# Seven products of quarters for the second matrix product of seven blocks, and a new order of steps

## The chip, the cores and the metric

The kernel runs on one core of a Trainium2 chip. The metric is the device time of one execution in microseconds (us), taken as the median of several runs. The core has a TensorE (PE; its weight loads are shown apart, as PEld), a VectorE (DVE), a ScalarE (ACT), a GpSimd (POOL) and a SyncE (SP), which here only issues transfers. Each engine works through its own queue of instructions in order, and waits on semaphores for the others. Memory on the chip is SBUF (128 partitions) and PSUM (eight banks of 512 float32 per partition), into which TensorE writes.

## The reference

```python
batch, n_heads, seq, head_dim = (8, 8, 576, 64)
scores = scale * np.matmul(q, k.transpose(0, 1, 3, 2))
gamma = 1.0 - 2.0 ** (-5.0 - np.arange(H, dtype=np.float32))
Dmat = np.where(rel >= 0, gamma[:, None, None] ** rel[None, :, :], 0.0)
attn = np.matmul(scores * Dmat[None, :, :, :], v)
x = attn.transpose(0, 2, 1, 3).reshape(B * S, H * D)      # 4608 x 512
h = x @ w_in                                              # 512 x 2048
s = np.sin(alpha * h)
g = h + s * s / (alpha + 1e-09)
out = g @ w_out                                           # 2048 x 512
```

A decaying attention without softmax over 8 batches of 576 positions feeds a two-layer network with a sine between its layers. Inputs and output are float32; the kernel multiplies in float16 with float32 sums.

## The kernel before

The 4608 rows of x are cut into nine blocks of 512. Block n below 8 holds the first 512 positions of batch n; block 8 holds the last 64 positions of all batches. (The title's and the text's blocks go from 0 to 8.)

For each batch the attention goes in chunks of 128 positions. `load` brings tiles of 256 positions, 512 KB each, to SBUF (for k and v of batches from `HALVED` = 5 on as four transfers), `cast` scales them by powers of gamma and rounds to float16, `turn` with `take` (batches 0 and 1, on TensorE and through PSUM) or `crossed` (a transposing DMA, batches 2 to 7) puts the head dimension on the partitions. `outer` makes the sums of k times v of the chunks, `evict`, `evict_bank` or `take_sum` bring them to SBUF, `more` and `to_state` carry the decayed state from chunk to chunk. `scores`, `masked` and `values` do the part inside a chunk, `add_states` adds what earlier chunks bring, and `keep` writes the result as float16, turned, into the block's x. `values` is made in two parts for two row halves of the array, and between them stands a wait: a drain of TensorE in batches 0 to 3, and a relay from there on (`told`: an empty instruction on POOL that waits for the first part, and for which the second waits). Class `Ends` does the same for the last 64 positions.

The network goes over 16 units of 128 hidden columns for each block. `project` (four matmuls of 512 columns) makes h of one unit in a PSUM bank, `sine` (ACT) makes the sine of it, `square` (DVE, ACT or POOL) squares it, and `product` (DVE) makes g = h + square times inverse of alpha as float16 in `gT`. `gemm2(n, u)` is a quarter of the sum for 128 rows of the output: four matmuls with a [128, 128] piece of g as weights and 512 columns of w_out moving, so 16 calls and 64 matmuls for a block. After four of them `finish` copies the bank to SBUF and stores it in two transfers of 64 rows each, because the rows of x stand in another order than the output's (even positions first, then odd).

The order of all steps is written out by hand up to block 3 and then made by loops over the units, with the second product of block n - 1 between the projections of block n, and the attention of block n + 1 at fixed units. PSUM is shared under fixed tags ("h0" to "h2", "op", and pairs "m0", "m1"), SBUF under tags with a few buffers each (six for `raw`): a load waits until a buffer is free. Dummy matmuls (`keep_busy`) stand at the start.

```python
for fk in range(4 * part, 4 * part + 4):
    matmul(
        ops[n, c, cols.start][:, cols], gT[n][:, fk, c * P : (c + 1) * P], w_out16[:, fk, cols],
        start=(fk == 0), stop=(fk == FC - 1), skip_group_check=True,
    )
```

Of the kernel before, what the change touches and what calls it, by code (L numbers as in the profile page):

```python
# [10 lines left out]
F32 = mybir.dt.float32  # L11
F16 = mybir.dt.float16
ADD = mybir.AluOpType.add
MULT = mybir.AluOpType.mult


@with_exitstack
def kernel(
# [10 lines left out]

# [9 lines left out]
    NBLK = NT // 512  # L44
    HALVED = 5
# [19 lines left out]
    work = ctx.enter_context(tc.tile_pool(name="w", bufs=1))  # L65
    psum = ctx.enter_context(tc.tile_pool(name="p", bufs=1, space=bass.MemoryType.PSUM))

    ident = const.tile([P, P], F16, tag="ident", bufs=1)
    mask = const.tile([P, 8 * 64], F16, tag="mask", bufs=1)
    cn = const.tile([P, 68], F32, tag="cn", bufs=1)  # L70
# [3 lines left out]
    eye = const.tile([16, 16], F32, tag="eye", bufs=1)  # L74
    alpha_r = const.tile([FC, P], F32, tag="alpha_r", bufs=1)
    alpha_t = const.tile([P, FC], F32, tag="alpha", bufs=1)
    inva = const.tile([P, FC], F32, tag="inva", bufs=1)
    w_in16 = const.tile([P, KT, FF], F16, tag="w_in16", bufs=1)
    w_out16 = const.tile([P, FC, 512], F16, tag="w_out16", bufs=1)
    sS = const.tile([P, B, 4, D], F16, tag="sS", bufs=1)  # L80
    xS = const.tile([P, KT, 512], F16, tag="xS", bufs=1)
# [4 lines left out]

    V, A_, G_ = nc.vector, nc.scalar, nc.gpsimd

    def load_w_in(g):
        cols = slice(g * 512, (g + 1) * 512)  # L90
        nc.gpsimd.dma_start(w_in16[:, :, cols], w_in_r[:, :, cols])

    def load_w_out(g):
        nc.gpsimd.dma_start(w_out16[:, 4 * g : 4 * g + 4, :], w_out_r[:, 4 * g : 4 * g + 4, :])
# [4 lines left out]
    def copy(eng, d_, s_):  # L99
        if eng is nc.scalar:  # L100
            eng.copy(d_, s_)  # L101
        else:
            eng.tensor_copy(d_, s_)  # L103

    raw = {}
    half = {}
    T = {}

    def load(b, nm, p):
        if p < 2 and b >= HALVED and nm != "q":  # L110
            t_ = work.tile([P, H, 2 * D], F32, tag="raw", bufs=6, name=nm + "32")
            for g in range(2):
                for r in range(2):
                    s0 = 256 * p + 128 * g + 64 * r
                    nc.sync.dma_start(  # L115
                        t_[halves(g), :, r * D : r * D + D], src[nm][b, :, s0 : s0 + 64, :].rearrange("h i d -> i h d")
                    )
        elif p < 2:
            t_ = work.tile([P, H, 2 * D], F32, tag="raw", bufs=6, name=nm + "32")
            nc.sync.dma_start(  # L120
                t_, src[nm][b, :, 256 * p : 256 * p + 256, :].rearrange("h (i r) d -> i h (r d)", r=2)
            )
        else:
            if b % 2 == 0:
                raw[b, nm, 2] = work.tile([P, H, D], F32, tag="raws", bufs=3, name=nm + "s32")
            t_ = raw[b - b % 2, nm, 2]
            nc.sync.dma_start(t_[halves(b % 2)], src[nm][b, :, 512:576, :].rearrange("h i d -> i h d"))
        raw[b, nm, p] = t_

    nbuf = {"k": 4, "q": 3, "v": 4}  # L130

    def cast(b, nm, p, eng, ys=(0, 1)):
        t_ = raw[b, nm, p]
        if (b, nm, p) not in half:
            if p < 2:
                d_ = work.tile([P, 16 * D], F16, tag=nm + "16", bufs=nbuf[nm], name=nm + "16")
                d_ = (
                    d_.rearrange("p (h r d) -> p h r d", r=2, d=D)
                    if nm == "v"
                    else d_.rearrange("p (a r t d) -> p a r t d", a=4, r=2, t=2)  # L140
                )
            elif nm == "v":
                d_ = work.tile([P, H, D], F16, tag="vs16", bufs=B // 2, name="vs16")
            else:
                d_ = work.tile([P, 4, 2, D], F16, tag="qks16", bufs=2, name=nm + "s16")
            half[b, nm, p] = d_
        dst = half[b, nm, p]
        if p == 2:
            if nm == "v":
                copy(eng, dst.rearrange("p h d -> p (h d)"), t_.rearrange("p h d -> p (h d)"))  # L150
            else:
                eng.tensor_tensor(  # L152
                    dst.rearrange("p a t d -> p t a d"),
                    t_.rearrange("p (t a) d -> p t a d", t=2),
                    fac_s[nm].rearrange("p (t a) -> p t a", t=2).unsqueeze(3).to_broadcast([P, 2, 4, D]),
                    MULT,
                )
        elif nm == "v":
            h0, h1 = 4 * ys[0], 4 * ys[-1] + 4
            copy(  # L160
                eng,
                dst[:, h0:h1].rearrange("p h r d -> p (h r d)"),
                t_[:, h0:h1].rearrange("p h x -> p (h x)"),
            )
        else:
            a0, a1 = 2 * ys[0], 2 * ys[-1] + 2
            n = 2 * (a1 - a0)
            eng.tensor_tensor(  # L168
                dst[:, a0:a1].rearrange("p a r t d -> p t (a r) d"),
                t_.rearrange("p (t a) x -> p t a x", t=2)[:, :, a0:a1].rearrange("p t a (r d) -> p t (a r) d", r=2),  # L170
                fac["halved k" if nm == "k" and b >= HALVED else nm]
                .rearrange("p (t x) -> p t x", t=2)[:, :, 2 * a0 : 2 * a1]
                .unsqueeze(3)
                .to_broadcast([P, 2, n, D]),
                MULT,
            )

    def new_T(b, nm, p):
        if (b, nm, p) not in T:
            T[b, nm, p] = (  # L180
                work.tile([P, 8, P], F16, tag=nm + "T", bufs=4, name=nm + "T")
                if p < 2
                else work.tile([P, 4, P], F16, tag=nm + "Ts", bufs=B // 2, name=nm + "Ts")
            )
        return T[b, nm, p]

    def crossed(b, p, nms="kq"):
        for nm in nms:
            x = half[b, nm, p]
            x = x.rearrange("p a r t d -> p (a r t d)") if p < 2 else x.rearrange("p a t d -> p (a t d)")  # L190
            nc.sync.dma_start_transpose(new_T(b, nm, p), x)

    trs = {}

    def turn(b, nm, p, tag, ys=(0, 1)):
        if (b, nm, p) not in trs:
            trs[b, nm, p] = psum.tile([P, 1024], F16, tag=tag, bufs=1, name="tr")
        tr, x = trs[b, nm, p], half[b, nm, p]
        for a in range(2 * ys[0], 2 * ys[-1] + 2):
            for r in range(2):  # L200
                matmul(  # L201
                    tr[:, 256 * a + 128 * r : 256 * a + 128 * r + 128],
                    x[:, a, r].rearrange("p t d -> p (t d)"),
                    ident,
                    start=(a == 0 and r == 0), stop=True, is_transpose=True, skip_group_check=True,
                )

    def take(b, nm, p, eng, ys=(0, 1)):
        d_ = new_T(b, nm, p).rearrange("p x n -> p (x n)")
        cols = slice(512 * ys[0], 512 * ys[-1] + 512)  # L210
        copy(eng, d_[:, cols], trs[b, nm, p][:, cols])

    def quads(firsts, seconds):
        return [(f, s) for s in seconds for f in firsts]

    matmul = nc.tensor.matmul

    open_turns = []

    def change_rows(key):  # L220

        if key in open_turns:
            nc.tensor.drain()
            open_turns.clear()
# [9 lines left out]
    def told(last, eng):  # L234

        mark = eng.nop()
        order(mark, last)
        return mark

    class Attention:  # L240
        def __init__(self, b):
            self.b = b
            self.halved = b >= HALVED
            self.both = {}
            self.o = {}
            self.ret = {}
            self.sc = {}
            self.kv = {}
            self.tiles = {}
            self.mark = {}  # L250

        def tile(self, name, shape, dtype, bufs):
            if name not in self.tiles:
                self.tiles[name] = work.tile(shape, dtype, tag=name, bufs=bufs, name=name)
            return self.tiles[name]

        @property
        def x(self):
            xs[self.b] = self.tile("xT", [P, KT, 512], F16, 3)
            return xs[self.b]  # L260

        @property
        def kvs(self):
            return self.tile("kvs", [P, 4, 4, D], F32, 1)

        def state_of(self, c):
            return self.tile("s16", [P, 3, 4, D], F16, 2)[:, c] if c < 3 else sS[:, self.b]

# [957 lines left out]
```

## Time and profile before

| what | us |
|---|---|
| median of 3 runs (308.53 to 311.25) | 309.3 |
| the profiled execution, its span | 309.4 |
| first projection begins | 25.4 |
| TensorE's last matmul ends | 305.9 |
| ScalarE busy in 144 sines | 97.1 |
| VectorE busy in 144 products (g) | 106.2 |
| TensorE busy in `gemm2`, 592 matmuls | 142.4 |

In a profile a line such as "L562 PE MATMUL ops<-w_out,gT 128*128 128x512 f16 x592 | 142.4, 374" names the line of the kernel, the engine, the operation, what is written from what, the shape, how many there were, and then the busy time in us and the mean of one in ns. After a second bar stands the time that the engine sat idle just before these instructions, and for what. Matmuls are pipelined, so the mean of one is longer than the time from one to the next; the latter is read from the starts. In a timeline a line begins with start and length in us. In a table of windows a line has the stretch, its length, the busy time and number of instructions of PE, PEld, DVE, ACT and POOL, the granted clock of TensorE, the share of time that the DMA engines were busy (over 1 where transfers overlap), and GB/s.

### The profile page before, as it was taken

The numbers are of one execution on the slowest core, as the hardware profiler recorded it, in microseconds if no ns is written. First come the engines' busy times: TensorE is split into PE (matmuls) and PEld (weight loads), VectorE is DVE, ScalarE is ACT, GpSimd is POOL, SyncE is SP. The second block draws the span as 40 slices with busy tenths as digits, with TensorE's granted clock in tenths as the row PEclk, the third lists the DMA queues.
The fourth block names the chain that finished last, engine by engine and source line by source line (L and its number), as shares of the span: only waits on it lengthen the run. The fifth ranks groups of instructions, "written<-read, shape, count | busy, mean of one in ns | idle before, by whom it ended". The sixth has DMA issues, their size and how long they took to land.

```text
span 309.4 us, 7922 instructions
## 1 busy us (share of the span) xinstructions
PE 296.4 (96%) x3257; PEld 150.9 (49%) x3257; DVE 207.4 (67%) x298; ACT 180.7 (58%) x286; POOL 138.4 (45%) x154
## 2 busy tenths in 40 slices
PE   6669999999999999999999999999999999999995
PEld 4546555554544544454445444544454454444443
DVE  1596799989859888666866586576656746655600
ACT  1434983766544766675677567756774456555411
POOL 5690774589449587759149722990030000000000
PEclk9776999999999999999999999999999999999999
DMA  7999999699497788987788788885431111111132
GB/s 227 335 215 217 278 260 247 160 247 303 90 289 213 88 190 183 272 140 171 161 226 209 179 163 192 230 199 132 101 72 39 34 36 36 35 34 37 42 89 73
DMA packets 115540, 49.84 MB, mean 161 GB/s; under 512 B 69792, under 2 KB 111024, under 8 KB 115504
## 3 DMA queue, kind: packets, MB, share of 16 engines
q1 hardware_dynamic: 110912, 44.97, 60.0%
q0 software_dynamic: 4224, 4.19, 8.1%
q8 instruction: 25, 0.41, 0.6%
q10 hardware_dynamic: 368, 0.18, 0.3%
q14 instruction: 11, 0.09, 0.1%
HBM read 36.74 MB, written 9.44 MB: 149 GB/s over the span
## 4 chain that ended last, share of the span: by engine, by line
PE 84%; DMA 3%; POOL 3%; SPq 3%; DVE 2%; ACT 1%; issue 1%; DVEq 0%; ACTq 0%; POOLq 0%
PE ops L562 39%; PE hps L519 37%; DMA q<-in_q_dram 3%; PE o L384 3%; PE sc L342 2%; SPq L115 2%; POOL q L168 1%; PE kv L282 1%; DVE s L316 1%; DVE ret L354 1%; PE o L406 1%; SPq L120 1%; ACT s_t L527 1%; POOL k L168 1%; PE tr L201 0%
## 5 line engine op out<-in xcount | busy, mean ns | idle before, releaser
L562 PE MATMUL ops<-w_out,gT 128*128 128x512 f16 (+2 forms) x592 | 142.4, 374 | 0.3 <-ACT kvs L101 0.2
L543 DVE SCALAR_TENSOR_TENSOR gT<-ss_t,inva,hps 128x512 f16<-128x512 f16 x144 | 106.2, 745 | 53.1 <-ACT ss_t L536 46.1
L527 ACT ACTIVATE s_t<-hps,alpha_t 128x512 f16<-128x512 f32 x144 | 97.1, 686 | 71.3 <-PE hps L519 68.8
L519 PE MATMUL hps<-xT,w_in 128*128 128x512 f16 (+1 forms) x544 | 127.7, 370 | 0.0
L519 PEld LDWEIGHTS <-w_in 128*128 128x128 f16 x608 | 59.1, 99 | 64.5 <-issue 0.9
L562 PEld LDWEIGHTS <-gT 128*128 128x128 f16 x592 | 56.2, 98 | 64.3 <-issue 0.7
L538 DVE TENSOR_TENSOR ss_t<-s_t 128x512 f16<-128x512 f16 x72 | 42.2, 587 | 19.5 <-ACT s_t L527 18.8
L536 ACT ACTIVATE ss_t<-s_t 128x512 f16<-128x512 f16 x62 | 38.8, 631 | 0.9
L354 DVE TENSOR_TENSOR ret<-sc,mask 128x1024 f16<-128x1024 f32 (+1 forms) x32 | 35.1, 1118 | 1.9 <-PE sc L342 1.8
L168 POOL TENSOR_TENSOR k<-k,cn 128x1024 f16<-128x1024 f32 (+1 forms) x13 | 22.1, 1699 | 25.0 <-DMA k<-in_k_dram 20.7
L101 ACT COPY osb<-ops 128x512 f32<-128x512 f32 (+1 forms) x34 | 19.7, 582 | 22.0 <-PE ops L562 20.6
L168 POOL TENSOR_TENSOR q<-q,cn 128x1024 f16<-128x1024 f32 (+1 forms) x16 | 27.2, 1708 | 10.1 <-DMA q<-in_q_dram 10.0
L538 POOL TENSOR_TENSOR ss_t<-s_t 128x512 f16<-128x512 f16 x10 | 10.8, 1083 | 19.5 <-ACT s_t L527 10.7
L101 ACT CAST xT<-o 128x1024 f16<-128x1024 f32 (+1 forms) x14 | 13.2, 958 | 7.9 <-PE o L406 7.8
L324 POOL TENSOR_TENSOR kvs<-s,kvs 128x256 f32<-128x256 f32 x22 | 16.1, 730 | 3.1 <-ACT kvs L101 1.4
L103 POOL CAST v<-v 128x1024 f16<-128x1024 f32 (+1 forms) x10 | 12.2, 1234 | 9.5 <-DMA v<-in_v_dram 8.4
L519 PE MATMUL hps<-xS,w_in 128*128 128x512 f16 x64 | 16.4, 379 | 0.0
L323 POOL TENSOR_TENSOR s<-kvs,cn 128x256 f32<-128x256 f32 x22 | 14.3, 651 | 0.3
L152 POOL TENSOR_TENSOR ks<-ks,cn 128x512 f16<-128x512 f32 x4 | 4.2, 1041 | 22.0 <-PE o L384 22.0
L384 PE MATMUL o<-ret,v 64*64 64x128 f16 (+1 forms) x512 | 11.9, 226 | 1.3 <-DVE ret L354 0.7
L342 PE MATMUL sc<-qT,kT 64*64 64x128 f16 (+1 forms) x512 | 10.9, 221 | 1.9 <-DVE ret L354 1.9
L316 POOL TENSOR_TENSOR s<-kvs,cn 128x256 f16<-128x256 f32 x19 | 12.2, 646 | 1.1 <-ACT kvs L101 0.5
(59 smaller groups left out, 142.3 us busy)
## 6 DMA issues: line engine op xcount, KB each, us to landing
out_dram<-osb SPq DMA_DIRECT2D x70, 128.0 KB, 2.4
q<-in_q_dram SPq DMA_DIRECT2D x16, 512.0 KB, 6.2
k<-in_k_dram SPq DMA_DIRECT2D x10, 512.0 KB, 8.2
v<-in_v_dram SPq DMA_DIRECT2D x10, 512.0 KB, 6.2
k<-in_k_dram SPq DMA_DIRECT2D x24, 128.0 KB, 3.1
v<-in_v_dram SPq DMA_DIRECT2D x24, 128.0 KB, 3.2
w_in<-in_moe_w_in_dram POOLq DMA_DIRECT2D x4, 512.0 KB, 11.3
w_out<-in_moe_w_out_dram POOLq DMA_DIRECT2D x4, 512.0 KB, 9.8
```

The source lines that it names most:

```text
L101: eng.copy(d_, s_)
L168: eng.tensor_tensor(dst[:, a0:a1].rearrange("p a r t d -> p t (a r) d"), t_.rearrange("p (t a) x -> p t a x", t=2)[:, :, a0:a1].rearrange( ...
L324: nc.gpsimd.tensor_tensor(self.kvs[:, c], s32, self.kvs[:, c], ADD)
L342: matmul(sc[halves(g), t, c : c + n], kT[halves(t), 2 * a + r, halves(g)], qT[halves(t), 2 * a : 2 * a + 2, 64 * g + i0 : 64 * g + 64], st ...
L354: nc.vector.tensor_tensor(ret.rearrange("p t (z x) -> p (t z) x", z=2)[:, :, 0:n], sc.rearrange("p t (z x) -> p (t z) x", z=2)[:, :, 0:n], ...
L384: made.append(matmul(o[t][halves(e), c : c + 128].rearrange("p (r i) -> p r i", r=2)[:, :, i0:64], v16[halves(g), 4 * t + 2 * x + e, r, :] ...
L519: matmul(hps_of[n, fc][0][:, cols], w_in16[:, a, fc * P : (fc + 1) * P], xs[n][:, a, cols], start=(a == 0 and part != 1), stop=(a == KT - ...
L527: nc.scalar.activation(s_t, hps, mybir.ActivationFunctionType.Sin, bias=0.0, scale=alpha_t[:, fc : fc + 1],)
L536: nc.scalar.activation(ss_t, s_t, mybir.ActivationFunctionType.Square)
L538: eng.tensor_tensor(ss_t, s_t, s_t, MULT)
L543: nc.vector.scalar_tensor_tensor(gT[n][:, fc, :], ss_t, inva[:, fc : fc + 1], hps, MULT, ADD)
L562: matmul(ops[n, c, cols.start][:, cols], gT[n][:, fk, c * P : (c + 1) * P], w_out16[:, fk, cols], start=(fk == 0), stop=(fk == FC - 1), sk ...
```

## The change

Three things change together.

First, in blocks 2 to 8 the product of g (512 x 2048) and w_out (2048 x 512) is made from quarters. Rows, inner dimension and columns are halved, and with A for g and B for w_out, seven products of 256 x 1024 by 1024 x 256 take the place of eight (Winograd's form): sums of quarters of A (S1 to S4, made anew for each block) and differences of quarters of B (T1 to T4, made once) go in, and the four quarters of the output are sums of the seven products. Part of these sums is made by letting products add up in one PSUM bank: bank X takes products 1, 6, 7 and 4 one after the other, and is read after each; bank Z takes 5 and then 3; bank Y takes 2.

```diff
+    def SM(n, s, i, eng):
+        i *= 4
+        S = {x: of_units(big16(f"S{x}.{n}"), i, 4) for x in (2, 3) if f"S{x}.{n}" in place}
+        S[1], S[4] = quarter_a(n, 1, 0, i, 4), quarter_a(n, 0, 1, i, 4)
+        a, b, op = {
+            1: lambda: (S[1], quarter_a(n, 1, 1, i, 4), ADD),
+            2: lambda: (S[1], quarter_a(n, 0, 0, i, 4), SUB),
+            3: lambda: (quarter_a(n, 0, 0, i, 4), S[1], SUB),
+            4: lambda: (S[4], S[2], SUB),
+        }[s]()
+        return eng.tensor_tensor(S[s], a, b, op)
+    BANK_OF = {1: "X", 6: "X", 7: "X", 4: "X", 2: "Y", 5: "Z", 3: "Z"}
+    def PP(n, p, j):
+        ps = bank(f"{BANK_OF[p]}.{n}")
+        for u in (2 * j, 2 * j + 1):
+            left, right = {
...
+            }[p]()
+            for c in range(2):
+                i = matmul(
+                    ps[:, 256 * c : 256 * c + 256], left[:, 0, 128 * c : 128 * c + 128], right[:, 0, :],
+                    start=starts(f"{BANK_OF[p]}.{n}"), stop=True, skip_group_check=True,
+                )
+        return i
+    KEPT = {2: ("Y", "p2"), 6: ("X", "u2"), 7: ("X", "u3"), 4: ("X", "c21")}
+    def CP(n, p, eng):
+        b, t = KEPT[p]
+        return copy(eng, mid32(f"{t}.{n}"), bank(f"{b}.{n}"))
+    SUMS = {11: ("X", "p2"), 22: ("Z", "u3"), 12: ("Z", "u2")}
+    def AD(n, c):
+        b, t = SUMS[c]
+        return nc.vector.tensor_tensor(mid32(f"{t}.{n}"), bank(f"{b}.{n}"), mid32(f"{t}.{n}"), ADD)
```

Second, the rows of x now stand in the output's order, because `values` and `add_states` write to PSUM with a step of two. A store is one transfer of 128 rows of 2 KB in blocks 0 and 1 (`OS`), and in blocks 2 to 8 one transfer of 256 rows of 1 KB for a quarter (`OQ`; in block 8 two of half the size).

```diff
-        return out[r0 : r0 + 128, :].rearrange("(i r) d -> r i d", r=2)
+        return out[576 * n + 128 * c : 576 * n + 128 * (c + m), :]
...
+    def OQ(n, c):
+        t = mid32(f"{dict(((11, 'p2'), (21, 'c21'), (22, 'u3'), (12, 'u2')))[c]}.{n}").rearrange("p (c d) -> p c d", c=2)
+        x = rows_of(n, 2 * (c // 10 - 1), 2)[..., 256 * (c % 10 - 1) : 256 * (c % 10)]
+        if n < 8:
+            return nc.sync.dma_start(x.rearrange("(c p) d -> p c d", p=P), t)
```

Third, the order, the engine of each movable step and the place of each buffer stand in one list, which a program found by a search in which every step takes its median time and nothing is delayed. The kernel reads the list and issues each step; an engine's queue holds its steps in the list's order. PSUM is one tile of eight banks, SBUF has 16 places of 4 KB (r4), 28 of 2 KB (h2) and 16 of 1 KB (s1) per partition. A piece of the list, and its end:

```diff
+PR.2.3.2 hps.2.3=2; MA.3.2:V s32.3.2=20; SI.2.0 s.2.0=0; CA.4.q.1.1:V q16.4.1=25; MB.3.2:G; PR.2.4.2 hps.2.4=3
+PD.2.2 gT.2=0; SI.2.3 s.2.3=11; SQ.2.0:V ss.2.0=4; G2.1.3.3; MA.3.3:G s32.3.3=13; SQ.2.3:A ss.2.3=7
...
+SM.8.1.1:V; PP.8.5.0 Z.8=2; CP.8.2:A p2.8=7; SM.8.2.1:G; PP.7.4.0; AD.8.11; PP.7.3.2; PP.7.4.1; SM.8.4.0:V; OQ.8.11
+PP.7.4.3; PP.8.6.0; PP.8.6.1; OQ.5.21; SM.8.4.1:V; PP.8.6.2; OQ.7.11; CP.7.4:V c21.7=23; PP.8.5.1; OQ.6.12; PP.8.6.3
+PP.8.5.2; OQ.3.12; CP.8.6:A u2.8=27; PP.7.3.3; OQ.7.22; PP.8.7.0; OQ.5.22; PP.8.7.2; PP.8.7.3; OQ.7.21; PP.7.3.1
+OQ.6.22; PP.8.7.1; PP.7.3.0; OQ.5.12; CP.8.7:A u3.8=13; PP.8.5.3; OQ.6.11; PP.8.4.3; AD.8.22; PP.8.4.0; AD.7.12
+PP.8.4.2; OQ.8.22; PP.8.4.1; PP.8.3.0; CP.8.4:A c21.8=0; OQ.7.12; PP.8.3.1; OQ.8.21; PP.8.3.3; PP.8.3.2; AD.8.12
+OQ.6.21; OQ.8.12
```

The names: LD load, CA cast, TU and TK turn and take, XP crossed, OU outer, EV and TS its evictions, MA and MB the two steps of `more`, ST to_state, SC scores, MK masked, VA and VB the two parts of values with RL the relay between them (now for every batch, on the engine named), SA add_states, KP keep, PR project, SI sine, SQ square, PD product, G2 gemm2 (blocks 0 and 1), FI and OS finish, TT and SM the differences and sums of quarters, PP a quarter of one of the seven products (four matmuls), CP and AD its evictions, OQ a quarter's store, LE, CE, XE and names with E in front the last 64 positions, KB dummies, WI and WO the loads of w_in and w_out. The number after the name is the block or batch; a letter after a colon is the engine (V VectorE, A ScalarE, G POOL), and "X.8=1" gives a buffer its place. There are 12 groups of dummies, 96 matmuls of 256 columns, where there were 28 of 256 or 512 and 44 of 64. Drains of TensorE between the two parts of `values` are gone.

More of the change, by code (lines that the diff above doesn't have):

```diff
@@ L73, with bank, big32, big16 @@
     g1 = cn[:, 48:52]
[L74 to L81, printed above, removed]
+    inva = fixed([P, FC], F32, "inva")
+    first = fixed([P, 1], F32, "first")
+    place = {}
+    def bank(name, n=1):
+        i = place[name]
+        return banks[:, i] if n == 1 else banks[:, i : i + n]
+    def big32(name):
+        return r4[:, place[name]]
+    def big16(name):
+        return r4[:, place[name]].bitcast(F16)
+    def mid16(name):
+        return h2[:, place[name]]
+    def mid32(name):
+        return h2[:, place[name]].bitcast(F32)
+    def small(name):
+        return s1[:, place[name]]
     src = {"q": q, "k": k, "v": v}
@@ L99, in copy @@
     def copy(eng, d_, s_):
[L100 to L176, printed above, removed]
@@ L193 @@
[L193 to L224, printed above, removed]
+        return eng.copy(d_, s_) if eng is nc.scalar else eng.tensor_copy(d_, s_)
@@ L541, in product @@
-    def product(n, fc):
-        hps, ss_t = hps_of.pop((n, fc))
-        nc.vector.scalar_tensor_tensor(gT[n][:, fc, :], ss_t, inva[:, fc : fc + 1], hps, MULT, ADD)
-    def rows_of(n, c):
-        if n == 8:
-            return out.rearrange("(b s) d -> b s d", s=S)[2 * c : 2 * c + 2, 512:576, :]
-        r0 = 576 * n + 128 * c
-        return out[r0 : r0 + 128, :].rearrange("(i r) d -> r i d", r=2)
-    def finish(n, c, eng=None, cols=slice(0, 512), issue=(nc.sync, nc.sync)):
-        osb = work.tile([P, 512], F32, tag="osb", bufs=4, name="osb")
-        copy(eng or nc.scalar, osb[:, cols], ops[n, c, cols.start][:, cols])
-        for r in range(2):
-            issue[r].dma_start(rows_of(n, c)[r, :, cols], osb[halves(r), cols])
@@ new lines, in rows_of, with G2 @@
+    def rows_of(n, c, m=1):
+        if n == 8:
+            return out.rearrange("(b s) d -> b s d", s=S)[2 * c : 2 * c + 2 * m, 512:576, :]
+        return out[576 * n + 128 * c : 576 * n + 128 * (c + m), :]
+    def G2(n, c, part):
+        for fk in range(4 * part, 4 * part + 4):
+            i = matmul(
+                bank(f"op.{n}.{c}"), g_of(n)[:, fk, c * P : (c + 1) * P], w_out16[:, fk, :],
+                start=starts(f"op.{n}.{c}"), stop=True, skip_group_check=True,
+            )
+        return i
```

1517 lines of the change are left out of this document (622 added, 895 removed).

## The prediction

> **What bounds the kernel now.** I read the page's busy shares first, then the busy time by windows.
>
> ```profile
> PE 296.4 (96%) x3257; PEld 150.9 (49%) x3257; DVE 207.4 (67%) x298; ACT 180.7 (58%) x286; POOL 138.4 (45%) x154
> ```
> ```profile
> 25.40:305.90 280.50, 279.62 (x2934) 138.07 (x2930) 192.25 (x281) 173.26 (x276) 120.86 (x125) 0.99 0.66 154
> 305.90:309.40 3.50, 0.00 (x0) 0.00 (x0) 0.33 (x1) 0.00 (x0) 0.00 (x0) 0.83 0.28 75
> 40.00:60.00 20.00, 19.72 (x309) 11.39 (x308) 19.31 (x31) 12.89 (x22) 12.23 (x12) 1.00 0.91 214
> 50.00:235.00 185.00, 184.56 (x2151) 90.60 (x2150) 135.82 (x187) 120.75 (x189) 106.73 (x110) 1.00 0.77 182
> 240.00:290.00 50.00, 49.93 (x352) 23.08 (x351) 30.27 (x50) 28.02 (x46) 0.00 (x0) 1.00 0.16 38
> ```
>
> The columns are stretch, length, busy time of PE, PEld, DVE, ACT and POOL, clock, DMA share, GB/s. From the first projection (25.4) to the last matmul (305.9) PE is busy for 279.6 of 280.5 us: TensorE sets the time, after a start of 25.4 and before an end of 3.5. VectorE may be as full as 19.31 of 20 without costing PE anything. The sum is made against this span, 309.4; the median of the runs is 309.3, so nothing has to be shifted.
>
> The start is bound by transfers:
>
> ```profile
> 12.00:30.00 18.00, 15.11 (x239) 10.21 (x240) 13.73 (x17) 6.39 (x10) 11.15 (x12) 0.64 1.19 235
> 30.00:50.00 20.00, 19.76 (x241) 11.24 (x239) 17.49 (x30) 15.78 (x28) 14.13 (x16) 1.00 1.18 263
> ```
> ```profile
> 11.82 1.68 POOL L91 DMA_DIRECT2D w_in<-in_moe_w_in_dram  x2
> 43.88 1.91 POOL L168 TENSOR_TENSOR k<-k,cn 128x1024 f16<-128x1024 f32 x1
> ```
> ```profile
> 25.37 3.34 PE L519 MATMUL hps<-xT,w_in 128*128 128x256 f16 x12
> 46.94 0.61 PE L201 MATMUL tr<-ident,k 128*128 128x128 f16 x8
> ```
>
> A DMA share of 1.19 and 1.18 says that the queues are full to 50 us.
>
> **The seven products (blocks 2 to 8).** G2 with 64 matmuls of 512 columns becomes 28 PP steps of four matmuls of 256 columns, 112 in all.
>
> ```profile
> 54.38 1.04 PE L519 MATMUL hps<-xT,w_in 128*128 128x256 f16 x8
> ```
> ```profile
> 55.03 1.03 PE L519 MATMUL hps<-xT,w_in 128*128 128x256 f16 x5
> ```
> ```profile
> 239.83 1.02 PE L519 MATMUL hps<-xT,w_in 128*128 128x512 f16 x4
> 245.01 1.02 PE L519 MATMUL hps<-xT,w_in 128*128 128x512 f16 x4
> ```
>
> Six groups of four wide matmuls lie between the last two rows: 5.18 / 24 = 0.216 us each. The seventh of the narrow ones starts 0.65 after the first (55.03 against 54.38, six steps): 0.109 us each, half. So columns are all that counts, and the weight loads stay hidden (PEld 138 of 280). A block costs 64 x 0.216 = 13.82 before and 112 x 0.109 = 12.21 after; seven blocks save 11.3 us. All of it lies on the path. The projections, scores, values and outer products keep their number.
>
> **What the products add elsewhere.** 56 sums of quarters (SM: 31 on VectorE, 25 on POOL), 8 differences of w_out (TT: 6 and 2), 28 evictions (CP: 21 on ScalarE, 7 on VectorE) in place of 28 of the old ones, and 21 additions from PSUM (AD, VectorE). Squares move: VectorE 72 to 32, ScalarE 62 to 77, POOL 10 to 35. The rows:
>
> ```profile
> L543 DVE SCALAR_TENSOR_TENSOR gT<-ss_t,inva,hps 128x512 f16<-128x512 f16 x95 | 70.1, 745 | 35.1 <-ACT ss_t L536 30.4 <-POOL ss_t L538 2.8
> L538 DVE TENSOR_TENSOR ss_t<-s_t 128x512 f16<-128x512 f16 x42 | 29.2, 698 | 9.6 <-ACT s_t L527 9.1
> L354 DVE TENSOR_TENSOR ret<-sc,mask 128x1024 f16<-128x1024 f32 x14 | 16.7, 1220 | 1.9 <-PE sc L342 1.8
> L103 DVE COPY osb<-ops 128x512 f32<-128x512 f32 x2 | 1.4, 678 | 0.0
> ```
> ```profile
> L538 DVE TENSOR_TENSOR ss_t<-s_t 128x512 f16<-128x512 f16 x24 | 10.2, 423 | 7.6 <-ACT s_t L527 7.4
> ```
> ```profile
> L538 POOL TENSOR_TENSOR ss_t<-s_t 128x512 f16<-128x512 f16 x10 | 10.8, 1083 | 19.5 <-ACT s_t L527 10.7 <-DVE gT L543 8.8
> ```
> ```profile
> 18.74 4.61 DVE L354 TENSOR_TENSOR ret<-sc,mask 128x1024 f16<-128x1024 f32 x4
> ```
> ```profile
> 195.49 0.54 PE L384 MATMUL o<-ret,v 64*64 64x128 f16 x32
> ...
> 197.66 0.39 PE L519 MATMUL hps<-xT,w_in 128*128 128x512 f16 x1
> ```
> ```profile
> L316 DVE TENSOR_TENSOR s<-kvs,cn 128x256 f16<-128x256 f32 x3 | 1.4, 473 | 0.8 <-POOL kvs L324 0.8
> ```
> ```profile
> L168 POOL TENSOR_TENSOR q<-q,cn 128x1024 f16<-128x1024 f32 x6 | 11.3, 1902 | 1.5 <-DMA q<-in_q_dram 1.5
> L316 POOL TENSOR_TENSOR s<-kvs,cn 128x256 f16<-128x256 f32 x11 | 7.4, 670 | 0.9 <-ACT kvs L101 0.5
> ```
> ```profile
> L527 ACT ACTIVATE s_t<-hps,alpha_t 128x512 f16<-128x512 f32 x96 | 64.8, 686 | 44.0 <-PE hps L519 41.6 <-DVE ret L354 1.1 <-DVE gT L543 1.0
> L536 ACT ACTIVATE ss_t<-s_t 128x512 f16<-128x512 f16 x48 | 29.9, 630 | 0.8
> ```
>
> The same square takes 423 ns after 235 us, where POOL is idle, and 698 before, where it is busy for 107 of 185 us: a delay of 0.275 for each VectorE step that reads two tiles of SBUF beside POOL, which an order made of medians does not hold. The product, which reads PSUM, stays at 745 to 748. [...]
>
> I lay the PE steps of the new list end to end at these pitches, and count the VectorE steps that stand among them. From PR.2.7.2 to PP.2.3.2 there are 24 PR and 4 G2 (24.2), 26 PP (11.3) and 13 attention steps (4.0, as seven took 2.17 from 195.49 to 197.66): 40 us of PE. VectorE has 59 steps: 22 PD (16.4), 6 MK (7.3), 7 SQ (3.0), 7 SM and TT (5.6: 0.8 each, an estimate from twice a square), 2 AD and 2 EV (2.8, as the PSUM copy of 678), 8 state steps (3.5, from the row of 473) and 5 casts (3.6, estimated as PSUM copies of like size): 42.2. Four MK in a row took 4.61, not 4.88, so a step hides some 0.06 of the one before: 38.7. But 27 of the 59 can meet POOL: plus 7.4 is 46.1 in a stretch of 40. Counted likewise, the 20 us from SC.2.0.1 come to 20.3, those from TU.1.q.1.2 to 21.2 and those from PR.5.13.2 to 21.4; the others stay below 19. VectorE thus owes 9.0 us. A lag is harmless until a PSUM bank is missed; with eight banks I let each of three crowded places run behind by one square and one product (1.4): some 5 us are left. Ends: 0 (every lag absorbed) and 16.8 (rival two).
>
> ScalarE's 25 sines and 11 squares come to 24 of the same 40 us, some 30 with its copies. POOL, by its rows (casts 1.90, squares 1.08, state steps 0.67, SM 2.0 as twice a square), has 25 of these 40, and 19 of 20 in its fullest stretch, from SM.4.2.0 on. Neither sets the time by itself.
>
> **The start.** Dummies rise from 28 wide or half-wide ones to 96, on an idle PE: nothing. Attention of block 0 is rearranged and could let projections start some 5 us sooner. But the second k tile of block 1 stands behind the same ten input tiles and weight loads in full queues; it was cast at 43.88 and turned at 46.94, 21.5 us of PE after the first projection. TU.1.k.1.2 stands 21.5 after the first PR too. What is won at 20 us is waited for there. I take 0; ends -5 (the transfers come sooner) and +4 (loads no longer held back by buffers delay the weights).
>
> **The end.**
>
> ```profile
> out_dram<-osb SPq DMA_DIRECT2D x70, 128.0 KB, 2.4
> ```
> ```profile
> GB/s 227 335 215 217 278 260 247 160 247 303 90 289 213 88 190 183 272 140 171 161 226 209 179 163 192 230 199 132 101 72 39 34 36 36 35 34 37 42 89 73
> ```
> ```profile
> 0.80 0.46 SPq L120 DMA_DIRECT2D k<-in_k_dram  x1
> ```
>
> In the new list 16 of the 28 stores of quarters (OQ, 256 KB) stand on SP's queue behind OQ.8.11, blocks 3 to 7 among them: no earlier one can leave before AD.8.11. 25 PP steps (10.9 us) follow that. 4.2 MB at the best mean of a slice, 335 GB/s, take 12.5 us; issuing 20 DMAs takes 20 x 0.5 = 10. With 1.9 us to land (2.4 less its own transfer) and the 1 us that the program still runs, the end is 5.5 after PE's, against 3.5 now: +2. The other bound is the stores' own rate, 38 GB/s at a share of 0.16 = 238 GB/s: 17.6 us, +7. I take the first, since those stores come from 64 partitions each and the loads, like the new stores, span 128; the ends are 0 (issue alone) and +7. [...]
>
> Stores of 128 rows instead of two of 64 halve SP's issues in between; no one waits there: 0. Values are written to PSUM with a step of two; no row shows it; each matmul writes as many elements: 0, ends 0 and +4. Relays (RL) replace PE drains; the nop queues behind POOL or VectorE, VB waits for it: other PE steps stand between in most places: 0, ends 0 and +3.
>
> **Sum.** 309.4 - 11.3 + 5 + 0 + 2 = 305.1; I say 305.
>
> **Rivals.** One: the order holds, VectorE's lags are absorbed and the end is bound by issue: 309.4 - 11.3 = 298. For it: 40 to 60 us with a full VectorE and a dense PE. Against: the 46.1 in 40.
>
> [...]
>
> Three: the stores' rate stays at 238 GB/s: 309.4 - 11.3 + 5 + 7 = 310. For it the only rows of stores; against it their 64 partitions.
>
> Four: the narrow matmuls do not save, as each brings a weight load: then 309.4 + 7 = 316. The rows of 256 columns speak against it.
>
> **Numbers.** About 1% (3.1 us) is what a measurement of this kernel can tell from no change. Forecast 0.45 (its own range 300 to 309), one 0.20, two 0.18, three 0.14, four 0.03. Faster takes rival one and three quarters of the forecast: 0.54. Same takes the rest of the forecast and rival three: 0.25. Slower takes two and four: 0.21. The range, 297 to 314, leaves out the outer halves of rivals one and two.
>
> **What will show it.** PE's matmuls: 784 of 256 columns at 0.109. [...] Squares on VectorE above 0.6 us on average. First projection before 25, a wait for k before TU.1.k.1.2. After PE's last matmul 5 to 6 us, with DMA near its full share: the end as reckoned; 10 or more: three. I am wrong if PE waits most for something else, as a relay or an X bank not yet read.

## The result and the profile after

The changed kernel takes 316.5 us (median of 4 runs, 315.8 to 318.0) against 308.9 (307.5 to 311.3): a ratio of 1.0255 with an interval of 1.0202 to 1.0308. It is slower by some 2.5%; 305 was predicted, at most 314. The profiled execution spans 314.7 us, against 309.4.

The page's row of busy shares, and groups of TensorE's instructions (line, tiles, shape, count, busy us, mean ns of one, idle time before them), after:

```profile
PE 299.6 (95%) x3601; PEld 189.9 (60%) x3601; DVE 260.7 (83%) x351; ACT 182.7 (58%) x300; POOL 199.5 (63%) x172
```
```profile
L855 PE MATMUL banks<-w_out,g 128*128 128x256 f16 x336 | 45.4, 273 | 1.0 <-DVE g L777 0.9
L573 PE MATMUL banks<-h 64*64 64x128 f16 (+1 forms) x512 | 18.5, 295 | 1.4 <-DVE g L777 0.9 <-issue 0.5
L542 PE MATMUL banks<-h 64*64 64x128 f16 (+1 forms) x512 | 11.7, 216 | 1.3 <-DVE g L777 0.9 <-DVE h L329 0.3
L606 PE MATMUL banks<-h 64*64 64x128 f16 x192 | 8.4, 306 | 0.0
```

And the same groups before, `values` and `add_states`:

```profile
L384 PE MATMUL o<-ret,v 64*64 64x128 f16 (+1 forms) x512 | 11.9, 226 | 1.3 <-DVE ret L354 0.7 <-POOLq L236 0.2
...
L406 PE MATMUL o<-qT,s 64*64 64x128 f16 x192 | 5.7, 229 | 0.0
```

TensorE is busier than before (299.6 against 296.4), though the seven products give it less to do. The reason stands in two rows: the 512 matmuls of `values` (L573) take 18.5 us where they took 11.9, and the 192 of `add_states` (L606) 8.4 where they took 5.7, 9.3 us in all. The scores (L542), of the same shape but written to PSUM without a step, take 11.7 (10.9 before). From one start to the next, after 28 us (where 448 and 168 of them lie), a matmul of `values` went from 16.0 to 29.6 ns and one of `add_states` from 19.0 to 32.2: (13.6 x 448 + 13.2 x 168) = 8.3 us. This holds what the new order does around these matmuls too; the experiments put the step alone at 7.0.

The runs below that differ in the step give the size for these 64x64 tiles: starts 1.5 to 1.75 times as far apart (16.0 to 26.4 and 19.0 to 33.2 ns from the kernel before to e2, 19.2 to 29.6 and 18.8 to 32.2 from e1 to the changed kernel). The prediction put it at 0.

Two marks divide the span: the turning of block 1's second k tile (the 46.94 row before) and TensorE's last matmul. The latter ends at 305.78 before, a little sooner than the 305.9 used above:

```profile
302.80 2.98 PE L562 MATMUL ops<-w_out,gT 128*128 128x320 f16 x27
```

Timeline and windows, after:

```profile
19.77 0.61 PE L754 MATMUL banks<-r,w_in 128*128 128x256 f16 x4
```
```profile
45.01 0.61 PE L465 MATMUL banks<-ident,h 128*128 128x128 f16 x8
```
```profile
305.81 1.15 PE L855 MATMUL banks<-r,g 128*128 128x256 f16 x9
306.79 1.91 PE L855 MATMUL banks<-w_out,g 128*128 128x256 f16 x16
```
```profile
308.70:314.70 6.00, 0.00 (x0) 0.00 (x0) 0.69 (x1) 0.00 (x0) 0.00 (x0) 0.67 0.67 208
95.70:140.40 44.70, 42.51 (x465) 24.85 (x464) 42.96 (x59) 28.95 (x47) 29.49 (x24) 1.00 0.86 191
45.01:308.70 263.69, 258.97 (x3093) 163.12 (x3091) 228.22 (x306) 158.36 (x259) 175.11 (x137) 1.00 0.61 140
```

| stretch | before | after | difference |
|---|---|---|---|
| to the second k tile | 46.94 | 45.01 | -1.9 |
| from there to the end of TensorE's last matmul | 258.84 | 263.69 | +4.9 |
| behind it | 3.7 | 6.0 | +2.3 |

To the first row belongs the granted clock. Its rows on the page, with a digit in tenths for each fortieth of the span, are shown here for before, after, and e2 (an experiment below whose start is that of the kernel before but for the step):

```profile
PEclk9776999999999999999999999999999999999999
```
```profile
PEclk9999999999999999999999999999999999999997
```
```profile
PEclk9799999999999999999999999999999999999999
```

From 12 to 30 us the clock was 0.64 before and 1.00 after. In e2 it was 0.91 from 0 to 20 us and 1.00 from 20 to 40, where the kernel before had 0.83 in both, and the second k tile was turned at 42.56. The start thus differs by 4.4 us between two executions with the old order of steps, and the 1.9 us can't be put down to the new one. Behind 46 us the clock is full in all three, so the middle stretch compares like with like.

What the middle stretch is made of, from each matmul's start to the next start, with waits of over 0.15 us put apart:

| middle stretch | before | after | difference |
|---|---|---|---|
| matmuls of the whole array | 234.8 | 226.9 | -7.9 |
| the attention's matmuls of 64x64 tiles | 23.6 | 31.9 | +8.4 |
| waits of over 0.15 us | 0.2 | 4.6 | +4.4 |

In the first of these rows the columns alone come to 10.4 us less: 11.3 for the seven products, as predicted, less 0.9 because four matmuls of 512 columns more of blocks 0 and 1 lie behind the k tile. What TensorE waited for in the whole span, after:

```profile
PE banks L790 <- DVE g L777: 1.9, 1, 1.9
PE banks L790 <- DVE h L555: 1.3, 1, 1.3
PE banks L411 <- DVE zero L365: 1.3, 1, 1.3
PE banks L542 <- DVE g L777: 0.9, 2, 0.7
PE banks L855 <- DVE g L777: 0.9, 1, 0.9
PE banks L573 <- DVE g L777: 0.9, 2, 0.5
```

Each row has the waiting tile and line, then the engine and tile waited for, us in all, times, and the longest. In the rows shown all but the start-up fill (zero, L365) wait for VectorE's products or masks. SyncE's issues at the end (start, length, line, count):

```profile
298.28 0.67 SPq L879 DMA_DIRECT2D out_dram<-h  x1
299.00 0.62 SPq L880 DMA_DIRECT2D out_dram<-h  x1
299.67 6.70 SPq L877 DMA_DIRECT2D out_dram<-h  x10
...
311.11 0.61 SPq L880 DMA_DIRECT2D out_dram<-h  x1
```

SyncE issues the 20 transfers without a pause from 298.28 to 311.72 (the last row's 311.11 and 0.61), 0.67 us each. The DMA engines are near full at the same time: from 306 to 309 us their share is 1.09, with 382 GB/s. The last store lands 3 us after its issue, at the end of the span.

### The profile page after: what moved, and what is told of

Its sections match the earlier page's. It is cut to its first block, busy times and chain, and to the rows that moved or that the text cites. A ratio compares the mean times of both kernels' runs of the same rounds, so it can differ in the third digit from the quotient of the medians.

```text
span 314.7 us, 8643 instructions
## 1 busy us (share of the span) xinstructions
PE 299.6 (95%) x3601; PEld 189.9 (60%) x3601; DVE 260.7 (83%) x351; ACT 182.7 (58%) x300; POOL 199.5 (63%) x172
## 4 chain that ended last, share of the span: by engine, by line
PE 78%; DVE 13%; issue 3%; POOL 2%; ACT 2%; POOLq 0%; DVEq 0%
PE banks L754 33%; PE banks L855 23%; PE banks L790 6%; DVE g L777 6%; PE banks L573 4%; PE banks L411 4%; PE banks L542 2%; PE banks L606 2%; DVE h L555 2%; PE banks L498 1%; ACT s L762 1%; DVE s L773 1%; DVE r L526 1%; PE banks L465 1%; POOL g L838 1%
## 5 line engine op out<-in xcount | busy, mean ns | idle before, releaser
L754 PE MATMUL banks<-r,w_in 128*128 128x512 f16 (+1 forms) x608 | 137.6, 368 | 0.4 <-DVE g L777 0.3
L762 ACT ACTIVATE s<-banks,alpha 128x512 f16<-128x512 f32 x144 | 95.1, 687 | 51.6 <-PE banks L754 49.5
L777 DVE SCALAR_TENSOR_TENSOR g<-s,inva,banks 128x512 f16<-128x512 f16 x144 | 102.1, 740 | 10.7 <-ACT s L772 6.8
L855 PEld LDWEIGHTS <-g 128*128 128x128 f16 x560 | 53.4, 98 | 17.0 <-DVE g L777 1.7
L773 POOL TENSOR_TENSOR s<-s 128x512 f16<-128x512 f16 x35 | 39.5, 1131 | 37.1 <-ACT s L762 34.6
L838 POOL TENSOR_TENSOR r<-g 128x1024 f16<-128x1024 f16 x18 | 39.9, 2221 | 22.2 <-DVE g L838 15.4
L447 POOL TENSOR_TENSOR h<-r,cn 128x1024 f16<-128x1024 f32 (+1 forms) x27 | 47.2, 1751 | 4.0 <-DMA r<-in_q_dram 3.7
L772 ACT ACTIVATE s<-s 128x512 f16<-128x512 f16 x77 | 47.2, 630 | 1.0
L855 PE MATMUL banks<-w_out,g 128*128 128x256 f16 x336 | 45.4, 273 | 1.0 <-DVE g L777 0.9
L555 DVE TENSOR_TENSOR h<-banks,mask 128x1024 f16<-128x1024 f32 (+1 forms) x32 | 35.3, 1117 | 4.3 <-PE banks L542 4.3
L790 PEld LDWEIGHTS <-g 128*128 128x128 f16 x128 | 11.6, 98 | 16.7 <-issue 4.9
L573 PE MATMUL banks<-h 64*64 64x128 f16 (+1 forms) x512 | 18.5, 295 | 1.4 <-DVE g L777 0.9
L526 POOL TENSOR_TENSOR r<-h,r 128x256 f32<-128x256 f32 x14 | 12.3, 875 | 10.9 <-DVE h L523 5.5
## 6 DMA issues: line engine op xcount, KB each, us to landing
r<-in_v_dram SPq DMA_DIRECT2D x24, 128.0 KB, 3.9
r<-in_k_dram SPq DMA_DIRECT2D x24, 128.0 KB, 3.3
```

Of the source, the lines that this page charges most:

```text
L447: return eng.tensor_tensor(dst[:, a0:a1].rearrange("p a r t d -> p t (a r) d"), t_.rearrange("p (t a) x -> p t a x", t=2)[:, :, a0:a1].rea ...
L555: return nc.vector.tensor_tensor(ret(b, p, y).rearrange("p t (z x) -> p (t z) x", z=2)[:, :, 0:n], bank(f"sc.{b}.{p}.{y}", 2).rearrange("p ...
L573: made.append(matmul(o[halves(e), t, c : c + 128].rearrange("p (i r) -> p r i", r=2)[:, :, i0:64], v16[halves(g), 4 * t + 2 * x + e, r, :] ...
L754: i = matmul(bank(hps)[:, cols], w_in16[:, a, u * P : (u + 1) * P], x_of(n)[:, a, cols], start=starts(hps), stop=(a == KT - 1), skip_group ...
L762: return nc.scalar.activation(small(f"s.{name}")[:, cols], bank(f"hps.{name}")[:, cols], mybir.ActivationFunctionType.Sin, bias=0.0, scale ...
L772: return nc.scalar.activation(ss_t, s_t, mybir.ActivationFunctionType.Square)
```

## The experiments

Theory A was that the step in the PSUM writes costs the 7 to 8 us that the prediction lacked. Its rivals were the end (stores on SyncE) and VectorE (its delay beside GpSimd, or its load). All ratios are to the kernel before, run on the same chip, with their intervals.

### The step taken away, and put into the kernel before

In the changed kernel, at both places where TensorE writes `o`:

```diff
-                            o[halves(e), t, c : c + 128].rearrange("p (i r) -> p r i", r=2)[:, :, i0:64],
+                            o[halves(e), t, c : c + 128].rearrange("p (r i) -> p r i", r=2)[:, :, i0:64],
```

> The changed kernel, but values and add_states write their columns of PSUM one after the other again instead of with a step of two; the stores are left, so within each 128 rows the output's rows come out in another order (even ones first). Theory A, the step makes each of these matmuls slower (29.6 ns from one to the next instead of 16.0 in values, 32.2 instead of 19.0 in add_states): back to about 16 and 19, TensorE ends some 8 us sooner, time about 308. Theory B, these steps are long because they wait in a tight order (relay, masks, VectorE): they stay near 29 ns, time 316 within 1.

309.3 us, ratio 1.002 (0.9975 to 1.0064). Groups of this kernel:

```profile
L573 PE MATMUL banks<-h 64*64 64x128 f16 (+1 forms) x512 | 11.9, 215 | 1.8 <-DVE g L777 0.9 <-issue 0.8
...
L606 PE MATMUL banks<-h 64*64 64x128 f16 x192 | 5.5, 219 | 0.0
```

Both rows are back where they were before the change, and so is the time: 2.3% of the 2.5 are gone, with the single stores left as they are. From starts, after 28 us, `values` is at 19.2 ns and `add_states` at 18.8, so the step costs (10.4 x 448 + 13.4 x 168) = 6.9 us in the changed kernel. The other direction puts the step, and single stores in blocks 0 to 7, into the kernel before:

```diff
-                                o[t][halves(e), c : c + 128].rearrange("p (r i) -> p r i", r=2)[:, :, i0:64],
+                                o[t][halves(e), c : c + 128].rearrange("p (i r) -> p r i", r=2)[:, :, i0:64],
...
-        return out[r0 : r0 + 128, :].rearrange("(i r) d -> r i d", r=2)
+        return out[r0 : r0 + 128, :]
```

> The kernel before, with this part of the change alone: values and add_states write with a step of two, and each finish of blocks 0 to 7 is one store of 128 rows. Theory A: the same matmuls slow from 16 and 19 ns to about 30, TensorE ends 7 to 8 us later, time 316. Theory B: nothing moves, 309 within 1. The single stores alone change less than 0.5 us in either, since block 8, which ends the kernel, is stored as before.

313.6 us, ratio 1.0144 (1.0063 to 1.0225). The groups:

```profile
L384 PE MATMUL o<-ret,v 64*64 64x128 f16 (+1 forms) x512 | 17.2, 296 | 1.0 <-DVE ret L354 0.5
...
L406 PE MATMUL o<-qT,s 64*64 64x128 f16 x192 | 8.4, 309 | 0.0
```

The rows grow by 8.0 us in a kernel without any of the products or the new order, and by starts (16.0 to 26.4 ns, 19.0 to 33.2) by 7.0. The time grows by 1.4%, some 4.5 us (1.9 to 7.0), and not by the 7 to 8 expected. The trace shows where the rest is:

```profile
42.56 0.61 PE L201 MATMUL tr<-ident,k 128*128 128x128 f16 x8
```
```profile
294.80 13.15 PE L565 MATMUL ops<-w_out,gT 128*128 128x512 f16 x76
```

From the second k tile to the last matmul's end (307.95) are 265.4 us against 258.8, 6.6 more; the start, with more of the clock as shown above, is 4.4 shorter, and the end is alike. Theory A stands: the step makes either kernel slower, by some 7 us of TensorE's time.

### The stores moved up

Twelve stores of blocks 3 to 7 went in the list from behind OQ.8.11 to just behind their sums.

> The changed kernel, with the 12 stores of quarters of blocks 3 to 7 that stood behind OQ.8.11 on SP's queue moved to where their sums are made. Theory: the end is bound by SP issuing 20 transfers at 0.65 us each; with 8 left the time after TensorE's last matmul falls from 6.0 to about 4 us, time 314.5. Rival, the end is bound by the last store alone (sum, issue, landing): it stays at 6.0, time 316.5.

316.1 us, ratio 1.0216 (1.0111 to 1.0322); the profiled execution spans 314.2. SyncE's last issues there:

```profile
310.15 0.59 SPq L887 DMA_DIRECT2D out_dram<-h  x1
310.79 0.62 SPq L888 DMA_DIRECT2D out_dram<-h  x1
```

The queue now pauses before 307 us, and the end shrinks only from 6.0 to 5.1 us (TensorE's last matmul ends at 309.1), between what theory and rival expected. What is left looks like a path: the last sum, two issues of 0.6 one behind the other, and the landing.

### The same turn at other places

The order of the rows must be turned somewhere. In `keep` (ScalarE or VectorE write the float16 copy with a step of two):

```diff
-                x_of(b)[:, :, cols].rearrange("p (t x) n -> p t x n", t=2),
-                bank(f"o.{b}.{p}", 2).rearrange("p t (x n) -> p t x n", x=2),
+                x_of(b)[:, :, cols].rearrange("p a (g i r) -> p a g r i", g=2, r=2),
+                bank(f"o.{b}.{p}", 2).rearrange("p t (x g r i) -> p (t x) g r i", x=2, g=2, r=2),
```

> As e1, but keep puts the rows in the output's order when it copies PSUM to SBUF (float16 written with a step of two by ScalarE and VectorE). [...] Rival, the step costs as much there: keep doubles, 12 full ones cost 13 us spread over two engines, time 309 to 312.

312.2 us, ratio 1.010 (1.0024 to 1.0176). ScalarE's copies here, and without the turn:

```profile
L329 ACT CAST r<-banks 128x1024 f16<-128x1024 f32 x8 | 10.4, 1314 | 6.9 <-PE banks L606 5.2 <-PE banks L573 1.6
```
```profile
L329 ACT CAST r<-banks 128x1024 f16<-128x1024 f32 x8 | 8.0, 1012 | 6.8 <-PE banks L606 5.0 <-PE banks L573 1.7
```

The stepped write costs ScalarE 30% as well (1314 against 1012 ns) and does not double keep, as the rival had it; on 8 such copies that is 2.4 us. By the ratios the kernel is 0.8% slower than e1, but the two intervals overlap. Or in the projection's reads:

```diff
+    def x_turned(n, a, cols):
+        x = x_of(n)[:, a, cols]
+        return x.rearrange("p (q r i) -> p q i r", r=2, i=64) if n < 8 else x
...
-                bank(hps)[:, cols], w_in16[:, a, u * P : (u + 1) * P], x_of(n)[:, a, cols],
+                bank(hps)[:, cols], w_in16[:, a, u * P : (u + 1) * P], x_turned(n, a, cols),
```

> The changed kernel with PSUM written without a step, as in e1, and the turn put into the projection's reads instead: its 512 matmuls of blocks 0 to 7 (of 512 columns, or in halves of 256) read the kept columns with a step of 64, so that the rows come out in the single stores' order. Theory A (only the write into PSUM is slow with a step): values stay at 19 ns from start to start, add_states at 19, a projection matmul of 512 columns at 216 to 224 ns as before, 309 to 310 us. Rival B (any stepped access of TensorE is slow): a projection matmul takes longer than 224 ns; each 10 ns more are 5 us, so over 314. Rival C (no part of the loss has to do with steps, the row order of the stores does): above 313 at unchanged matmuls.

438.1 us, ratio 1.408 (1.402 to 1.415). The projection's group here, and in the changed kernel:

```profile
L758 PE MATMUL banks<-r,w_in 128*128 128x512 f16 x544 | 258.6, 614 | 0.0
```
```profile
L754 PE MATMUL banks<-r,w_in 128*128 128x512 f16 x544 | 130.6, 379 | 0.4 <-DVE g L777 0.3
```

Rival B is right: these stepped reads are slow, as the stepped writes of e2 were: 128.0 us more for the 480 turned matmuls among them, 0.267 each, so 0.48 us where 0.216 do without the step.

### What VectorE holds up

With the step gone (e1) TensorE still waits, and the products' saving still doesn't show: from the second k tile (43.45) to the last matmul's end (302.83) e1 takes 259.4 us, 0.5 more than before. In it the waits of over 0.15 us come to 6.8. The longest waits of e1, by line:

```profile
PE banks L754 <- DVE g L777: 3.2, 3, 2.3
PE banks L790 <- DVE g L777: 1.9, 1, 1.9
PE banks L790 <- DVE h L555: 1.3, 1, 1.3
```

Three kernels on top of e1 tried its cause. The squares of GpSimd (`SQ...:G` to `SQ...:A` in the list):

> e1 (no step in PSUM, rows in another order within each 128) with the 35 squares of GpSimd moved to ScalarE, at their places in the list. GpSimd loses 39.5 us of work, ScalarE gains 35 x 0.63 = 22. [...] Rival S (VectorE's own sum of work in the stretches 40 to 60 and 160 to 200 us is the bound): waits and time as in e1, 308.5 to 309.5. Rival R (ScalarE comes late with 22 us more): waits for s on VectorE grow, over 310.

308.7 us, ratio 0.9948 (0.9900 to 0.9995). VectorE's squares fall from 619 to 571 ns and TensorE's waits behind the k tile from 6.8 to 3.6 us, so VectorE's squares are shorter beside a GpSimd without squares; the time is 2 us below e1's by the ratios, but the two intervals overlap. The squares of VectorE (`:V` to `:A`):

> e1 with the 32 squares of VectorE moved to ScalarE, at their places in the list; GpSimd's stay. VectorE loses 19.7 us, ScalarE gains 20. Theory S (VectorE's sum of work is what TensorE waits for in 40 to 60 and 160 to 200 us): waits for g fall by more than half, 304 to 305 us. [...] Rival R (ScalarE comes late): over 310.

312.2 us, ratio 1.0064 (1.0021 to 1.0107). The sums of quarters left out:

```diff
     def SM(n, s, i, eng):
+        return None
...
-                6: lambda: (of_units(big16(f"S2.{n}"), u, 1), of_units(big16("T2"), u, 1)),
-                7: lambda: (of_units(big16(f"S3.{n}"), u, 1), quarter_b(0, 1, u, 1)),
+                6: lambda: (quarter_a(n, 0, 0, u, 1), of_units(big16("T2"), u, 1)),
+                7: lambda: (quarter_a(n, 0, 0, u, 1), quarter_b(0, 1, u, 1)),
```

> e1 without the 56 sums of the hidden layer's quarters (SM; the products read the quarters themselves, so blocks 2 to 8 come out otherwise; TensorE's instructions are the same). VectorE loses some 30 us of work, GpSimd some 53. Theory S (TensorE's remaining waits are VectorE's sum of work, to which the sums are added): TensorE's waits for g, 6 to 7 us in e1, fall under 2 us, and the seven products show their saving: 301 to 304 us, a ratio of 0.975 to 0.985. Rival (the waits come from the order of the list, whatever VectorE's load): waits of 5 us and more stay, 307 to 309.

307.5 us, ratio 0.9966 (0.9931 to 1.0002). TensorE's waits without the sums, and VectorE's products with its squares on ScalarE (e10):

```profile
PE banks L754 <- DVE g L777: 2.4, 3, 1.5
PE banks L790 <- DVE g L777: 1.9, 1, 1.9
PE banks L790 <- DVE h L555: 1.3, 1, 1.3
```
```profile
L786 DVE SCALAR_TENSOR_TENSOR g<-s,inva,banks 128x512 f16<-128x512 f16 x144 | 101.8, 740 | 33.3 <-ACT s L781 27.4 <-POOL s L782 5.8
```

Theory S falls in e14. Without the sums VectorE is busy for 230.0 us instead of 261.1, and GpSimd for 142.0 instead of 200.7. Still TensorE's waits behind the k tile come to 5.1 us (6.8 in e1), and at most some 1.7 us are gained by the ratios, whose intervals overlap. Two of the longest waits (1.9 and 1.3, for G2 of block 0) stand at 38 to 51 us, before any product of quarters. e10 can't decide about S: there VectorE waits 27.4 us for ScalarE in its products, where it waited 5.7 in e1, as rival R had it. Moving GpSimd's squares seemed to gain 2 us in e8, but the pair below didn't repeat it. That most of the waiting lies in the order, and not in one engine's load or in VectorE's delay beside GpSimd, is what is left; it is not shown, as no order was made anew.

### Versions that keep the output's order of rows

Plain writes, and the turn in the stores as before (two of 64 partitions each), with the early stores:

```diff
+            x = x.rearrange("(c i r) d -> r i c d", r=2, i=64)
+        else:
+            x = x.rearrange("(c r) s d -> r s c d", r=2)
+        nc.sync.dma_start(x[0], t[halves(0)])
+        return nc.sync.dma_start(x[1], t[halves(1)])
```

> PSUM written without a step and the turn left to the stores, as in the kernel before: each product's quarter goes out in two stores of every other row, 64 partitions each, and so do the blocks of eight products. With it the twelve late stores moved up to behind their sums (as in e3) and GpSimd's 35 squares on ScalarE (as in e8). If the stepped write is the only loss of the single stores and the two moves keep what they gave alone (e8: 0.995 of the time before; e3: 0.5 us less than the changed kernel): 306 to 308 us, a ratio of 0.985 to 0.995, values at 18 to 19 ns. Rival D (28 more stores of 0.6 us on SyncE's queue make the loads behind them late): PE waits for loads or casts in blocks 3 to 7, 310 to 313. Rival E (the end is bound by the transfers of 64 partitions): end more than 7 us behind TensorE's last matmul, 309 to 311.

> The same with GpSimd's squares left where the change has them. Theory L (GpSimd's squares hold up VectorE, and so TensorE): 2 us slower than with the squares on ScalarE, 308 to 310. Rival S (VectorE's sum of work): the same time within 0.5 us.

> As the first of these three, but of block 8's four pairs of stores the second is issued by ScalarE and not by SyncE. If the end is bound by SyncE issuing one store after the other at 0.6 us, the pair goes out together: 0.6 us less behind TensorE's last matmul. Rival (the end is a fixed path of a sum, one store's issue and landing, 0.7 + 0.6 + 2.4 us and what closes the program): the same time within 0.5 us.

> The kernel with two stores, early stores and the last stores on two queues, with all 144 squares on ScalarE (35 fewer on GpSimd as before in it, and now 32 fewer on VectorE too, 18 to 20 us). Theory S: TensorE's waits for g fall by half against that kernel, 2 to 3 us faster, a ratio near 0.995. Rival R (VectorE then waits for ScalarE's squares, as in e10, where 27 us of such waiting stood): no faster, a ratio of 1.00 to 1.01.

The four came to 1.0104 (1.0062 to 1.0146), 1.0105 (1.0066 to 1.0144), 1.0046 (1.0000 to 1.0093) and 1.0170 (1.0113 to 1.0226). The first missed its 306 to 308 us: it took 311.8, in rival D's range. GpSimd waits 30.1 us for input tiles there, where it waited 19.6 in e8, and TensorE's waits behind the k tile are 6.7 us where they were 3.6. That fits D (more stores on SyncE's queue, loads later), but no run tests it alone. The first two are equal, so GpSimd's squares were not worth 2 us here. The third's end is 4.6 us (matmuls to 301.7, span 306.3) against 6.0 in the first, more than the 0.6 expected. SyncE's issues at that end:

```profile
299.63 0.59 SPq L891 DMA_DIRECT2D out_dram<-h  x1
300.28 0.61 SPq L892 DMA_DIRECT2D out_dram<-h  x1
300.94 2.12 SPq L891 DMA_DIRECT2D out_dram<-h  x3
```

The firsts of the last three pairs follow each other at (2.12 - 0.6) / 2 = 0.76 us, and ScalarE issues the seconds beside them. The fourth goes the way of its rival R, and further than the 1.00 to 1.01 given: VectorE waits 36.6 us for ScalarE in its products, and TensorE for both. No version here that keeps the output's order beats the kernel before.

## Why the prediction was wrong

The step that failed is "Values are written to PSUM with a step of two; no row shows it; each matmul writes as many elements: 0, ends 0 and +4." The cost is 7.0 us by starts (6.9 in e1's comparison, 7.0 in e2's), outside its ends of 0 and +4. The argument counted elements; these matmuls start 1.5 to 1.75 times as far apart when they write with a step. Without the step the time falls to 309.3, inside the range, but no faster than before: the step is the largest part of the error and not the whole. From the forecast's 305.1 to the span of 314.7 lead the step (+7.0), more changes between kinds of matmuls with short waits (+3.9, not in the sum), the four matmuls more in the middle stretch (+0.9), the waits (-0.6), the start (-1.9) and the end (+0.3). The other terms:

- **The products, -11.3.** Right: 784 matmuls of 256 columns at 0.109 (9 of them lie between the starts 305.81 and 306.79). Rival four is out.
- **VectorE, +5.** The size was about right: TensorE's waits of over 0.15 us behind the second k tile come to 4.6 us, against 0.2 before, and 2.2 more lie shortly ahead of it. Of the predicted stretch (PR.2.7.2 to PP.2.3.2, 95.7 to 140.4) 42.51 of 44.70 us are busy, and 2.1 are such waits; in e1 it takes 41.9, near the 40 laid out. The waits of 1.9 and 0.3 at 40 to 44 us and of 0.9 at 85 to 86 stand in two other stretches that were counted as crowded (from TU.1.q.1.2 and SC.2.0.1). The one of 1.3 at 50.96 was not named, and the stretch from PR.5.13.2 has none. (Eight state steps at 473 ns are 3.8 us, not 3.5, which changes little.) The squares took 685 ns, above 600 as said:

```profile
L773 DVE TENSOR_TENSOR s<-s 128x512 f16<-128x512 f16 x32 | 21.8, 685 | 5.7 <-ACT s L762 4.6 <-POOL s L773 1.0
```

- **The start, 0.** The first projection came at 19.77, below 25, and most of it was given back by the second k tile: 1.9 us are left, inside the ends. But no wait for k stands there: TensorE waits 2.2 us for VectorE's products instead. And the clock differs between the two profiles, which the prediction did not weigh though its own row has 0.64. Whether the 96 dummies, put at nothing, keep the clock up is not shown.
- **The end, +2.** It is +2.3: 6.0 us where 5 to 6 stood, with the DMA engines near full, as said. SyncE's issues fill the same time, at 0.67 us each and not 0.5, so the trace doesn't tell the two bounds apart. That 64 partitions held the old stores to 238 GB/s, on which the choice between the two rates rested, no run shows; from 306 to 309 us the new ones moved 382. The terms listed (12.5 - 10.9 + 1.9 + 1) add up to 4.5 and not 5.5; one us of the working has no name. Rival three is out.
- **Relays, 0.** At most 0.5 us (the wait for an issue in L573's row).
- **Not in the sum.** TensorE changes more often between small and large matmuls: in the middle stretch 38 times each way where it was 25. A large matmul before a small one takes some 0.1 us longer to the next start (0.31 instead of 0.216 at 512 columns), and from a group's last small one to the next large one pass 0.14 us on average before, and 0.19 with the step in the changed kernel. These changes and the short waits around them are the +3.9: 2.5 in the row of the whole array (-7.9 against -10.4) and 1.4 in that of the attention (8.4 against 7.0).

The middle stretch then is -10.4 (columns), +7.0 (step), +4.4 (waits) and +3.9 (changes and short waits): the +4.9 measured. No run shows the 16.8 us that VectorE's term had as its upper end (rival two): TensorE's waits grew by these 4.4 us, and moving GpSimd's squares gained some 2 us (e8) or nothing (e11 and e12).

## What to carry to other kernels

When a change turns the order of elements inside a matmul's output or moving operand, look first at how far apart consecutive elements lie, not at how many there are, and price it by the nearest group with and without a step. Here the turn cost some 0.8% of the time in a few copies or in the stores (e4 and e12 against e1), 2.3% in the writes to PSUM and 40% in the projection's reads. And a saving on the bounding engine has to be counted together with the order that comes with it: here 11 us of columns were real, and changes between kinds of matmuls, waits and the end took them back even without the step. Last, look at the granted clock before two starts are compared: here the same old order differed by 4.4 us.

## What the runs showed of the hardware

- A PSUM write of float32 with a step of two made matmuls of 64x64 tiles (`values`, mostly of 128 columns) start 26.4 ns apart instead of 16.0 in the kernel before (e2), and 29.6 instead of 19.2 in the changed kernel (e1).
- A moving operand of float16 read with a step of 64 elements made a matmul of 512 columns take 0.48 us (e7) instead of 0.216.
- SyncE issued one store after the other 0.63 to 0.72 us apart, whether it carried 128 or 256 KB (the changed kernel from 298.28 us on, e11 at its end).
- ScalarE's copy of 128x1024 from PSUM to float16 took 1314 ns with a step of two in its write and 1012 without (e4 and e1).
